# The seventh tile's logits and routing, moved from two to six steps into the eighth tile's matmuls

## Chip, cores and metric

The kernel runs on one core of a Trainium2 chip. The metric is the device time of one execution in microseconds (us).

## The reference, cut to what matters

Three stages follow each other: attention over two sequences of 576 tokens, a dense MLP with a cosine gate, and a second MLP in which every token goes to one of eight experts. The change lies where the second matmul of the dense MLP meets the routing of the second MLP.

```python
h = x @ w_in                      # 1152 x 512 by 512 x 2048
g = h * np.cos(h)
x = g @ w_out                     # 1152 x 2048 by 2048 x 512
logits = x @ w_gate               # 1152 x 8
expert_idx = np.argmax(logits, axis=1)
...
if counts[e] < capacity:
    disp[e, counts[e]] = x[i]     # token i takes the next place of its expert
...
h = np.maximum(np.einsum('ecd,edf->ecf', disp, w1), 0.0)
y = np.einsum('ecf,efd->ecd', h, w2)
out[i] = gate_w[i] * y[expert_idx[i], pos[i]]
```

## The kernel before, in words

The 1152 tokens are nine tiles of 128, counted here as first to ninth; the code counts them T = 0 to 8. `l2_wide` does the matmuls of `g @ w_out` for the first five tiles together. `l2r` does the other four one after the other and lays the routing of all nine tiles in between. A tile has 48 matmuls (L867, three for each of 16 blocks), which `l2r` takes in eight steps of six. After them `l2_end` empties the bank: ACT writes the row (L858) and, for the eighth and ninth tile, also a 32-bit copy `xq` (L856); DVE writes the row's low half (L859).

Routing a tile has two parts.

- `route_a` turns the tile. For the first seven tiles SP issues a transposing DMA, `xr` from `row` (L895). For the eighth and ninth (T >= NDT, NDT = 7), TensorE transposes `xq` (L900) and ACT copies the result (L902).
- `route_b` forms the logits on TensorE (L917 with `xr`, L914 with `xq`); DVE finds the largest (L927, L929, L930) and the one-hot row `roh` (L931); TensorE sums the places (L934 to L936); ACT forms the probability (L928, L937); DVE finds the row number `rsli` (L938 to L942), the weight (L943 to L945) and the new counts `cnt` (L946); POOL scatters the row to the table `disp` in device memory with an indirect DMA (L947).

In `l2r` a tile's `route_b` comes at the first step that lies at least `RD` = 2 steps behind its `route_a`. The seventh tile's `route_a` stands at step 16 (of 0 to 31), which is the first step of the eighth tile. Before the eighth tile's `route_b` stands `hook`: it copies the counts (L1310), and SP fetches the first 144 rows of two experts back from `disp`, turned (`eX`, L1013), with their weights and token numbers (`eM`, L1020). These fetches wait until the seventh tile's scatter has landed. After the eighth tile's `route_b`, `partial` picks the next expert (L1166 to L1175), and SP loads its number into a register (L1170).

Experts are worked in slots. The weights of a slot are eight chunks of 512 KB, fetched on SP's queue into the staging buffers `ws` (L969 for w1, L973 for w2), and each is split by ACT (L658) and then by DVE (L659) into two halves. There are three staging buffers here, so that a chunk is fetched when the chunk three places before it has been split. The chunks of the second slot are called 1 to 8 below, those of the third slot 9 to 16. Behind chunk 8 SP's queue holds the fetches of `hook`, then the register load L1170, then chunk 9.

Behind the ninth tile's matmuls TensorE starts on the two experts' first 144 rows: 12 matmuls a block (L1044), eight blocks for the first expert, then four for the second, then the first expert's second layer (L1066, four blocks of 24). A block takes the next of six PSUM banks (tags s, pt and mm, two of each); ACT (L1046) and DVE (L1047) empty it. In between lie the ninth tile's routing and `counts` (L1181 to L1206), which needs the ninth tile's `cnt`. Then comes a branch by size, and the rest of the experts.

The Python text gives the order in which work is issued. The framework's scheduler then sets the row of instructions on each engine by its own estimate of times, and every engine works its row in that order.

Of the kernel before, what the change touches and what calls it, by code (L numbers as in the profile page):

```python
# [51 lines left out]
MR = 8  # L52
RP = 2
RD = 2
RF = 2
W2P = 24
CYCLE = (
# [13 lines left out]
NDT = 7  # L71
# [6 lines left out]
def kernel(ctx, tc, q, k, v, s, w_in, w_out, wg, w1, w2, out, cap, wide):  # L78
# [802 lines left out]
    def l2(tiles):  # L881
        for T in tiles:
            xp = bank(L2T) if T == tiles[0] else bank("mm")
            for f in range(KF):
                l2_mm(xp, T, f)
                if f % 2 == 1:
                    if f == KF - 1:
                        l2_end(T, xp)
                    yield

    def route_a(T):
        r, xf = rows[T]
        if T < NDT:
            xr = work.tile([128, 2 * KD, 128], F16, tag="xr", name="xr", bufs=2)
            nc.sync.dma_start_transpose(out=xr, in_=r[:, 0:DM].bitcast(F16))  # L895
            rows[T] = (r, xr)
        else:
            tp = bank("pt")
            for kk in range(KD):
                nc.tensor.transpose(tp[:, kk * 128:(kk + 1) * 128], xf[:, kk * 128:(kk + 1) * 128], idf)  # L900
            xt = xq[:, DM:2 * DM].rearrange("p (k t) -> p k t", k=KD)
            nc.scalar.copy(xt.rearrange("p k t -> p (k t)"), tp)  # L902
            rows[T] = (r, xt)
# [103 lines left out]
    def e_rows(e, ns, rows_):  # L1007
        i = eb["n"]
        eb["n"] += 1
        n16 = -(-ns // 16) * 16  # L1010
        xo = i % XR * 2 * KD * 224 if ns <= 224 else i % 2 * 2 * KD * n16
        X = eb["X"][:, xo:xo + 2 * KD * n16].rearrange("p (k n) -> p k n", k=2 * KD)
        nc.sync.dma_start_transpose(out=X, in_=rows_[0:n16, 0:DM].bitcast(F16))  # L1013
        ex_[e] = (X, i)
# [8 lines left out]
    def at(src, off, ns):  # L1023
        n16 = -(-ns // 16) * 16
        return disp[bass.ds(src * NS if off is None else off, n16), :]
# [63 lines left out]
    def run(*gens):  # L1089
        live = [[g, n, 0.0] for g, n in gens]  # L1090
        while live:
            live.sort(key=lambda z: z[2])
            z = live[0]
            try:
                next(z[0])
                z[2] += 1.0 / z[1]
            except StopIteration:
                live.remove(z)

    def take(gen, n):  # L1100
        for _ in range(n):
            next(gen, None)
            yield

    def seq(*gens):
        for g in gens:
            yield from g

    def l2r(tiles, hook):
        gen = l2(tiles)  # L1110
        pend = list(range(tiles[0]))
        mid = []
        step = 0

        def finish():
            R_ = mid.pop(0)[0]
            if R_ == HTILE:
                hook()
            route_b(R_)
            if R_ in (PTILE, HTILE):  # L1120
                partial()

        for T in tiles:
            for j in range(KF // 2):
                next(gen)
                if mid and step - mid[0][1] >= RD:
                    finish()
                if pend and step % RP == 0:
                    mid.append((pend[0], step))
                    route_a(pend.pop(0))  # L1130
                step += 1
                yield
            pend.append(T)
        for T in pend:
            while mid and len(mid) >= 1:
                finish()
            mid.append((T, step))
            route_a(T)
        yield
        finish()  # L1140
        yield
# [15 lines left out]
    def partial():  # L1157
        V = nc.vector
        pp = bank("sm", 2)
        nc.tensor.matmul(pp[:, 0:E], lhsT=onesm, rhs=cnt[:, 0, :], start=True, stop=True)  # L1160
        ky = work.tile([1, E], F32, tag="ky", name="ky", bufs=1)
        so = work.tile([1, E], F32, tag="so", name="so", bufs=1)
        si = work.tile([1, 1], I32, name="psi", bufs=2)
        pick, keys = P["pick"], P["keys"]
        i = len(P["o"])
        V.scalar_tensor_tensor(ky, pp[0:1, 0:E], float(E), keys, ALU.mult, ALU.add)  # L1166
        V.max(so, ky)
        V.tensor_copy(si, so[:, 0:1])
        V.tensor_scalar(si, si, E - 1, E - 1, ALU.bitwise_and, ALU.bitwise_xor)
        P["o"].append(nc.values_load(si, engines=SP, min_val=0, max_val=E - 1))  # L1170
        if i < NH:
            V.tensor_copy(P["row"][:, i:i + 1], si)
            V.tensor_scalar(P["row"][:, i:i + 1], P["row"][:, i:i + 1], float(NS), None, ALU.mult)
        V.tensor_scalar(pick[:, i, :], ky, so[:, 0:1], None, ALU.is_equal)
        V.scalar_tensor_tensor(keys, pick[:, i, :], -1e9, keys, ALU.mult, ALU.add)  # L1175
# [121 lines left out]
    with ExitStack():  # L1297
        if True:
# [10 lines left out]
            def hook():  # L1309
                nc.vector.tensor_copy(cnt0, cnt[:, 0, :])  # L1310
                for h in range(NH):
                    e_rows(h, HEAD, at(P["o"][h], None, HEAD))
                    e_meta(h, HEAD, at(P["o"][h], None, HEAD))

            def ahead(steps):
# [6 lines left out]
                while k < 2 * items:  # L1322
                    next(pre)
                    k += 1

            tail = l2r(range(WN, NTILE), hook)
            lead = (NTILE - WN) * KF // 2 + 1
            run((take(tail, lead), lead), (ahead(lead), lead))
            ws[0:0] = [xa.tile([128, 1024], F32, name=f"ws{3 + i}") for i in range(NST)]
            phase, phase1 = (expert(h, HEAD, "out0", ex_.pop(h)) for h in range(NH))  # L1330
            for _ in range(RF):
                next(phase)
# [5 lines left out]
            for h in range(NH):  # L1338
                n = max(p[h] for p in PROFILES)
                e_rows(h, n, at(P["o"][h], first[h], n))  # L1340
            run((seq(take(phase, KE - RF), take(phase1, LA), phase, phase1), 2 * (KE + KD)), (take(pre, items), W3P))
            level = nc.values_load(regs[0], min_val=0, max_val=len(LIMITS))
# [42 lines left out]
```

## Time and profile before

| | us |
|---|---|
| median of three runs | 432.86 |
| lowest and highest of them | 428.65, 433.86 |
| the profiled execution | 430.29 |
| its span in the trace | 428.2 |
| PE busy | 395.1 (92%) |
| DVE busy | 311.8 (73%) |
| ACT busy | 274.8 (64%) |
| POOL busy | 149.2 (35%) |

The profiled execution's time is its span and 2.1 us that lie around it. PE is TensorE's matmuls, DVE the vector engine, ACT the scalar engine, POOL GpSimd, SP the engine whose queue issues the DMAs. The shares are means over a program whose stages have different limits; the stage of the change lies between 264 and 325 us of the span.

### The profile page before, as it was taken

The page shows a single profiled execution, that of the slowest core. Times are in us where ns is not written, and L with a number is a line of the kernel's source. Part 1 is how long each engine was busy: PE and PEld are TensorE (multiplying, and loading weights), DVE is VectorE, ACT ScalarE, POOL GpSimd, SP SyncE. Part 2 cuts the span into 40 slices and gives each one's busy share as a digit, 9 for nine tenths or more (in the row PEclk, how much of TensorE's full clock was granted, in tenths as well). Part 3 has the DMA queues.
Part 4 walks back from the last instruction along what each step waited for, and adds up shares of the span by engine and source line. Part 5 has one row for each costly group of instructions (what it writes and reads, how often), then busy time and mean ns, then how long its engine had stood idle before and what let it go on. Part 6 is the DMA issues. An engine that isn't in the chain of part 4 may idle for free.

```text
span 428.2 us, 10640 instructions
## 1 busy us (share of the span) xinstructions
PE 395.1 (92%) x3928; PEld 281.6 (66%) x3928; DVE 311.8 (73%) x768; ACT 274.8 (64%) x630; POOL 149.2 (35%) x261
## 2 busy tenths in 40 slices
PE   2799999999999999999999999797998999999783
PEld 2588888886666666654444454354997999987552
DVE  7769999749999599989885664672842477877670
ACT  6679989986878677775234532533734477777560
POOL 7668887563554445455000032010011011122100
PEclk9989999999999999999999999899999999999998
DMA  7979795203369932323667456947759298998851
GB/s 166 210 173 190 165 203 151 72 2 100 98 188 328 369 124 92 88 70 98 183 204 230 116 128 206 280 110 222 252 148 216 61 314 264 308 330 265 264 209 30
DMA packets 90003, 77.38 MB, mean 181 GB/s; under 512 B 62768, under 2 KB 70960, under 8 KB 89942
## 3 DMA queue, kind: packets, MB, share of 16 engines
q1 hardware_dynamic: 86934, 71.62, 59.5%
q0 software_dynamic: 1952, 4.73, 3.2%
q8 instruction: 33, 0.54, 0.5%
q10 hardware_dynamic: 1056, 0.26, 0.3%
q14 instruction: 28, 0.23, 0.2%
HBM read 57.66 MB, written 12.28 MB: 163 GB/s over the span
## 4 chain that ended last, share of the span: by engine, by line
PE 32%; DMA 9%; DVE 7%; issue 5%; ACT 4%; SPq 2%; POOL 1%; POOLq 0%; ACTq 0%; DVEq 0%
DMA ws<-in_moe_w_dram 8%; PE ps_mm L867 7%; PE ps_sm L867 5%; PE ps_pt L1044 3%; PE ps_s L1066 3%; PE ps_mm L1044 2%; PE ps_s L867 2%; PE ps_pt L867 2%; PE ps_s L1044 2%; PE ps_pt L1066 2%; PE ps_mm L1066 2%; DVE gall L659 1%; ACT gall L658 1%; DVE y L818 1%; SPq L1013 1%
## 5 line engine op out<-in xcount | busy, mean ns | idle before, releaser
L812 PEld LDWEIGHTS <-win 128*128 128x128 f16 x576 | 56.3, 98 | 37.0
L867 PEld LDWEIGHTS <-gall 128*128 128x128 f16 x432 | 41.3, 98 | 49.3 <-issue 2.5
L867 PE MATMUL ps_mm<-wout,gall 128*128 128x512 f16 x240 | 57.9, 387 | 0.3 <-DVE n__2954 L826 0.3
L659 DVE SCALAR_TENSOR_TENSOR gall<-ws,gall 128x1024 f16<-128x1024 f32 x32 | 38.8, 1221 | 23.2 <-ACT gall L658 22.1
L1053 POOL DMA_INDIRECT out_dram<-gall,eM x15 | 18.8, 1252 | 98.4 <-ACT gall L1052 77.4
L658 ACT ACTIVATE gall<-ws 128x1024 f16<-128x1024 f32 x32 | 33.7, 1056 | 26.8 <-DMA ws<-in_moe_w_dram 26.8
L658 ACT ACTIVATE wout<-ws 128x512 f16<-128x512 f32 (+1 forms) x32 | 27.3, 860 | 23.7 <-DVE ws L681 18.5
L241 ACT ACTIVATE z<-z,st 128x256 f32<-128x256 f32 (+4 forms) x72 | 41.9, 586 | 0.7 <-DVE st L241 0.7
L947 POOL DMA_INDIRECT disp<-row,rsli x9 | 9.2, 1017 | 94.0 <-ACT rm L928 48.5
L241 DVE CUSTOM_DVE_ANT_0 z<-ps_s,zm 128x512 f32<-128x512 f32 (+3 forms) x72 | 34.5, 511 | 10.0 <-PE ps_s L244 8.8
L659 DVE SCALAR_TENSOR_TENSOR wout<-ws,wout 128x512 f16<-128x512 f32 (+1 forms) x32 | 30.4, 955 | 8.2 <-ACT wout L658 8.0
L812 PE MATMUL ps_s<-xT,win 128*128 128x384 f16 x192 | 34.2, 326 | 0.0
L812 PE MATMUL ps_pt<-xT,win 128*128 128x384 f16 x192 | 33.8, 326 | 0.0
L812 PE MATMUL ps_mm<-xT,win 128*128 128x384 f16 x192 | 33.8, 326 | 0.0
L247 PE MATMUL ps_pt<-idf,z 128*128 128x128 f32 x192 | 30.2, 282 | 1.3 <-DVE p L241 1.3
L1044 PEld LDWEIGHTS <-gall 128*128 128x128 f16 x480 | 27.0, 97 | 3.7 <-issue 1.9
L825 ACT ACTIVATE y<-y,quarter 128x384 f32<-128x384 f32 x48 | 29.2, 609 | 0.1
L241 ACT COPY p<-ps_pt 128x512 f32<-128x512 f32 (+2 forms) x48 | 25.2, 525 | 5.9 <-PE ps_pt L247 5.5
L659 DVE SCALAR_TENSOR_TENSOR win<-ws,win 128x1024 f16<-128x1024 f32 x16 | 19.4, 1225 | 11.7 <-ACT win L658 11.7
L247 PEld LDWEIGHTS ps_pt<-idf,z 128*128 128x128 f32 x192 | 23.1, 144 | 6.3 <-issue 1.5
L244 PE MATMUL ps_s<-kT,qT 128*128 128x384 f16 (+7 forms) x128 | 23.9, 307 | 1.1 <-DMA kT<-bt 0.6
L658 ACT ACTIVATE win<-ws 128x1024 f16<-128x1024 f32 x16 | 16.8, 1055 | 10.9 <-DMA ws<-in_moe_w_dram 10.9
(495 smaller groups left out, 891.9 us busy)
## 6 DMA issues: line engine op xcount, KB each, us to landing
ws<-in_moe_w_dram SPq DMA_DIRECT2D x64, 512.0 KB
ws<-in_moe_w_in_dram SPq DMA_DIRECT2D x16, 512.0 KB
ws<-in_moe_w_out_dram SPq DMA_DIRECT2D x16, 512.0 KB
disp<-zc SPq DMA_DIRECT2D x18, 257.0 KB
out_dram<-zc SPq DMA_DIRECT2D x9, 256.0 KB
qf<-in_q_dram SPq DMA_DIRECT2D x16, 128.0 KB
vf<-in_v_dram SPq DMA_DIRECT2D x16, 128.0 KB
kf<-in_k_dram SPq DMA_DIRECT2D x14, 128.0 KB
```

The lines of the kernel that those rows point to most:

```text
L241: return pin(f(*a, **kw))
L244: return pin(nc.tensor.matmul(out_, **kw))
L247: return pin(nc.tensor.transpose(out_, in_, id_))
L658: nc.scalar.activation(hi, src, AF.Copy, scale=sc)
L659: (eng or nc.vector).scalar_tensor_tensor(lo, src, sc, hi, ALU.mult, ALU.subtract)
L812: nc.tensor.matmul(hp[:, 0:CH], lhsT=win[a][:, kk, fs], rhs=xT[:, x_, kk, xs], start=(n == 0), stop=(n == 3 * KD - 1))
L825: nc.scalar.activation(y, y, AF.Sin, scale=TWO_PI, bias=quarter)
L867: gate["pe"] = nc.tensor.matmul(xp, lhsT=G[c][:, a, f, ts], rhs=wout[w_][:, f, :], start=(f == 0 and n == 0), stop=(f == KF - 1 and n == 2))
L947: sc = nc.gpsimd.indirect_dma_start(out=disp, out_offset=bass.IndirectOffsetOnAxis(ap=sli.bitcast(U32), axis=0), in_=r, in_offset=None, bo ...
L1044: gate["pe"] = nc.tensor.matmul(hp[:, 0:ns], lhsT=a1[:, kk, a, fs], rhs=X[:, x_ * KD + kk, 0:ns], start=(n == 0), stop=(n == 3 * KD - 1))
L1053: sc = nc.gpsimd.indirect_dma_start(out=out, out_offset=bass.IndirectOffsetOnAxis(ap=M[:, b, 1:2].bitcast(U32), axis=0), in_=y, in_offset= ...
L1066: nc.tensor.matmul(yp[:, 0:ns], lhsT=a2[:, f, w_, d * 128:(d + 1) * 128], rhs=Hh[:, a, f, :], start=(n == 0), stop=(n == 3 * KE - 1))
```

## The change

For the seventh tile alone (T = NDT - 1), `route_b` comes six steps behind `route_a` and not two, so at step 22 in place of step 18. Nothing is added or left out.

```diff
 RD = 2
+RL = 6
 RF = 2
...
                 next(gen)
-                if mid and step - mid[0][1] >= RD:
+                if mid and step - mid[0][1] >= (RL if mid[0][0] == NDT - 1 else RD):
                     finish()
```

The new line shifts the numbers behind it by one, so that L659 before is L660 after. On TensorE's row the seventh tile's twelve logit matmuls stand behind 24 matmuls counted from the place where the row of before has its L934, and not behind 7. The scheduler then orders DVE, ACT and POOL anew between this place and the branch; SP's row stays as it was, instruction for instruction.

DVE, the seventh tile's routing from the one-hot row on. Before:

```order
L931 TENSOR_SCALAR roh<-rw,rm 128x8
L946 TENSOR_TENSOR cnt<-cnt,roh 128x8
L1310 COPY cnt_84<-cnt 128x8
L938 TENSOR_SCALAR rt_3894<-ps_sm 128x8
L659 SCALAR_TENSOR_TENSOR gall<-ws_92,gall 128x2x512
L939 TENSOR_TENSOR rt_3894<-rt_3894,ps_sm 128x8
L943 TENSOR_SCALAR rm<-rm 128x1
L940 TENSOR_TENSOR rt_3894<-rt_3894,roh 128x8
L944 RECIPROCAL rm<-rm 128x1
L942 TENSOR_REDUCE rsli<-rt_3894 128x1
L659 SCALAR_TENSOR_TENSOR gall<-ws_90,gall 128x2x512
L945 TENSOR_SCALAR row<-rm 128x1
```

And in the changed kernel:

```order
L660 SCALAR_TENSOR_TENSOR gall<-ws_91,gall 128x2x512
L932 TENSOR_SCALAR roh<-rw,rm 128x8
L944 TENSOR_SCALAR rm<-rm 128x1
L860 SCALAR_TENSOR_TENSOR row<-ps_mm,row 128x512
L939 TENSOR_SCALAR rt_3918<-ps_sm 128x8
L945 RECIPROCAL rm<-rm 128x1
L947 TENSOR_TENSOR cnt<-cnt,roh 128x8
L940 TENSOR_TENSOR rt_3918<-rt_3918,ps_sm 128x8
L946 TENSOR_SCALAR row<-rm 128x1
L660 SCALAR_TENSOR_TENSOR gall<-ws_92,gall 128x2x512
L941 TENSOR_TENSOR rt_3918<-rt_3918,roh 128x8
L943 TENSOR_REDUCE rsli<-rt_3918 128x1
```

Before, the splits in this piece are those of chunks 5 (ws_92) and 6 (ws_90), and 7 and 8 come behind it. Now the split of chunk 7 (ws_91) stands ahead of the one-hot row, and the split of chunk 8 (the second ws_92) ahead of the last two steps to the row number `rsli`, without which POOL can't scatter.

ACT, from the last tile's 32-bit copy `xq` on. Before:

```order
L658 ACTIVATE gall<-ws_90 128x1024
L856 ACTIVATE xq<-ps_mm 128x512
L858 ACTIVATE row<-ps_mm 128x512
L658 ACTIVATE gall<-ws_91 128x1024
L902 COPY xq<-ps_pt 128x512
L658 ACTIVATE gall<-ws_92 128x1024
L1046 ACTIVATE eH<-ps_s 128x144
```

And in the changed kernel:

```order
L857 ACTIVATE xq<-ps_mm 128x512
L859 ACTIVATE row<-ps_mm 128x512
L903 COPY xq<-ps_pt 128x512
L1047 ACTIVATE eH<-ps_s 128x144
L659 ACTIVATE gall<-ws_90 128x1024
L1047 ACTIVATE eH<-ps_pt 128x144
```

The splits of chunks 9 to 11 (ws_90, ws_91, ws_92 here) stood ahead of the ninth tile's three evacuations and the first expert block's; now these four come first.

DVE, around the release of the first experts' banks. Before:

```order
L659 SCALAR_TENSOR_TENSOR gall<-ws_92,gall 128x1024
L1047 SCALAR_TENSOR_TENSOR eH<-ps_s,eH 128x144
L1047 SCALAR_TENSOR_TENSOR eH<-ps_pt,eH 128x144
L930 TENSOR_REDUCE rm<-rw 128x1
L943 TENSOR_SCALAR rm<-rm 128x1
L1047 SCALAR_TENSOR_TENSOR eH<-ps_mm,eH 128x144
L931 TENSOR_SCALAR roh<-rw,rm 128x8
L659 SCALAR_TENSOR_TENSOR gall<-ws_90,gall 128x1024
```

And in the changed kernel:

```order
L660 SCALAR_TENSOR_TENSOR gall<-ws_92,gall 128x1024
L943 TENSOR_REDUCE rsli<-rt_4130 128x1
L946 TENSOR_SCALAR row<-rm 128x1
L1191 MAX so<-ky 1x8
L1195 TENSOR_TENSOR pr<-ps_sm,pick 1x8
L1192 CAST si<-so 1x8
L1195 TENSOR_TENSOR pr<-ps_sm,pick 1x8
L1193 TENSOR_SCALAR si<-si 1x8
L1197 TENSOR_TENSOR pr<-ps_sm,pick 1x8 x3
L1198 COPY ky<-so 1x5
L1048 SCALAR_TENSOR_TENSOR eH<-ps_mm,eH 128x144
L660 SCALAR_TENSOR_TENSOR gall<-ws_90,gall 128x1024
```

Both pieces go from the split of chunk 11 to that of chunk 12. Before, three expert blocks are emptied in between and the ninth tile's counts come later; now the counts' arithmetic stands there, and only the third block (bank mm) is emptied. Elsewhere on this row the ninth tile's `cnt` now stands behind the split of chunk 9, and the second expert's first four blocks behind those of chunks 13 to 16; before, two of the four came ahead of chunk 13.

## Rows read from the trace of the kernel before

**Rows 1.** Stretches: us, then PE, PEld, DVE, ACT, POOL busy, clock, DMA share, GB/s.

```profile
271.50:274.10 2.60, 0.01 (x1) 0.00 (x0) 0.60 (x1) 1.03 (x1) 0.00 (x0) 1.00 1.08 306
274.50:277.50 3.00, 3.00 (x12) 1.08 (x9) 1.90 (x7) 1.99 (x5) 0.00 (x0) 0.50 0.95 266
...
293.70:296.70 3.00, 0.05 (x2) 0.02 (x1) 0.52 (x1) 1.61 (x3) 0.00 (x0) 1.00 0.93 329
296.70:306.80 10.10, 10.09 (x149) 9.80 (x150) 9.39 (x45) 6.89 (x17) 0.97 (x1) 1.00 0.88 280
340.70:410.00 69.30, 62.90 (x855) 56.36 (x851) 49.60 (x73) 49.88 (x91) 12.09 (x8) 1.00 0.88 288
```

**Rows 2.** Timeline of PE: start, us, instruction, count, [idle before <- releaser].

```profile
263.10 6.85 PE L867 MATMUL ps_mm<-wout,gall 128*128 128x512 f16 x31
269.79 0.17 PE L934 MATMUL ps_sm<-ebrow,onesm 128*128 128x16 f16 x1
...
274.13 0.46 PE L917 MATMUL ps_s<-wgs,xr 128*128 128x8 f16 x12 [2.62 <-ACT gall L658]
274.45 3.77 PE L867 MATMUL ps_mm<-wout,gall 128*128 128x512 f16 x9
278.05 0.17 PE L936 MATMUL ps_sm<-roh,tri 128*128 128x16 f16 x1
...
282.83 2.75 PE L867 MATMUL ps_mm<-wout,gall 128*128 128x512 f16 x12
...
292.82 0.91 PE L1044 MATMUL ps_s<-eX,win 128*128 128x144 f16 x12
296.68 0.65 PE L900 MATMUL ps_pt<-idf,xq 128*128 128x128 f32 x4 [2.95 <-ACT xq L856]
...
306.06 0.91 PE L1044 MATMUL ps_mm<-eX,gall 128*128 128x144 f16 x12
306.81 1.66 PE L1066 MATMUL ps_s<-eH,win 128*128 128x144 f16 x24
```

**Rows 3.** The chain that ended last, 281 to 297 us: start, us, what.

```profile
281.12 0.16 DVE row L945
...
282.08 3.22 DMA disp<-row,rsli
...
285.38 2.24 SPq L1013
...
291.45 3.62 DMA ws<-in_moe_w_dram
...
296.05 0.59 ACT xq L856
```

**Rows 4.** Timeline of ACT, same columns as rows 2.

```profile
275.70 1.06 ACT L658 ACTIVATE gall<-ws 128x1024 f16<-128x1024 f32 x1
...
279.06 1.06 ACT L658 ACTIVATE gall<-ws 128x1024 f16<-128x1024 f32 x1 [0.98 <-DMA ws<-in_moe_w_dram]
...
283.33 1.06 ACT L658 ACTIVATE gall<-ws 128x1024 f16<-128x1024 f32 x1 [0.94 <-DMA ws<-in_moe_w_dram]
...
299.13 1.06 ACT L658 ACTIVATE gall<-ws 128x1024 f16<-128x1024 f32 x1 [0.59 <-DMA ws<-in_moe_w_dram]
```

**Rows 5.** Timeline of DVE, same columns.

```profile
274.15 1.23 DVE L659 SCALAR_TENSOR_TENSOR gall<-ws,gall 128x1024 f16<-128x1024 f32 x1 [2.06 <-ACT gall L658]
...
278.37 1.22 DVE L659 SCALAR_TENSOR_TENSOR gall<-ws,gall 128x1024 f16<-128x1024 f32 x1
...
304.15 0.16 DVE L942 TENSOR_REDUCE rsli<-rt 128x1 int32<-128x8 f32 x1
...
304.97 0.29 DVE L1047 SCALAR_TENSOR_TENSOR eH<-ps_pt,eH 128x144 f16<-128x144 f32 x1
...
309.08 4.61 DVE L659 SCALAR_TENSOR_TENSOR gall<-ws,gall 128x1024 f16<-128x1024 f32 x4
```

**Rows 6.** SP's own waits, 324 to 341 us: us in total, times, longest.

```profile
SPq L1013 <- PE ps_pt L1044: 7.5, 2, 4.9
```

## The prediction

> **What bounds the kernel now.** I read the busy table by stretch first, then PE's timeline, then the chain that ended last, then ACT and DVE in the same stretch. The reader is to see two pauses of PE. From 271.5 to 274.1 it does nothing [rows 1]: it stands before the seventh tile's logits, which wait for the transposing DMA of `xr`; they start at 274.13 after 2.62 us [rows 2]. Behind this pause the granted clock is 0.50 from 274.5 to 277.5 [rows 1], and nine matmuls take from 274.45 to 278.05, 3.60 us [rows 2]. The second pause, 2.95 us before 296.68, ends with ACT's `xq` L856 [rows 2]; after it the clock stays at 1.00 [rows 1].
>
> The chain says why the second one is there [rows 3]. DVE finishes the seventh tile's row at 281.28, POOL's scatter starts at 282.08 and lands 3.22 us on, SP's fetch of `eX` starts at 285.38 and, behind it on the queue, that of chunk 9 at 291.45; chunk 9 is there at about 295.1, and ACT, which has its split ahead of the ninth tile's `xq`, only then comes to the `xq` at 296.05. So what binds here is a line of waits through DVE, POOL and SP's queue, and the seventh tile's scatter is its head. From 296.7 to 306.8 PE is busy 10.09 of 10.10 us [rows 1].
>
> **What the change takes away.** 31 matmuls start within 263.10 to 269.79 [rows 2], 0.216 us each. The logits now stand 24 matmuls behind 269.79: 269.79 + 24 x 0.216 = 274.97. SP's row is unchanged, so `xr` still lands at about 274.13, 0.84 us earlier. The first pause (2.62 us) goes, and with it the nine slow matmuls' excess, 3.60 - 9 x 0.216 = 1.66 us. On ACT the ninth tile's evacuations now come ahead of chunk 9, so the second pause (2.95 us) goes too. Sum: 7.2 us of PE time. It counts only where nothing else is late.
>
> **What is late next: the scatter.** Each engine works its row in order, so I follow DVE's new row. Chunk 7 may be fetched when chunk 4 is split; that split starts at 274.15 and stays, so ACT still starts on chunk 7 at 279.06 [rows 4, 5], and DVE splits it from 280.15 to 281.38 (1.06 and 1.23 us). Now the one-hot row stands behind this split: 281.5. The eighth tile's `xq`, also behind chunk 7 on ACT, starts at 280.0. PE has done the six matmuls of the ninth tile that stand ahead of the transposes by 277.9, waits for `xq` until 280.65, and again for the one-hot row until 281.6, because L936 now stands among the transposes. So PE comes back to the ninth tile at 281.95, not 282.83 [rows 2]: of the 4.3 us that the first pause and its slow matmuls gave, 0.9 are left.
>
> DVE goes on: the eighth tile's row half (0.69 us), five small steps to 282.6, then the split of chunk 8. Its fetch follows the split of chunk 5, which DVE started at 278.37 [rows 5], behind a step that waited for PE. Nothing of the routing stands ahead of it now, and ACT began on chunk 5 at 275.70 or earlier [rows 4], so DVE starts between 275.4 and 276.8; I take 276.3. Before, 283.33 - 279.59 = 3.74 us lay between that split's end and ACT on chunk 8 [rows 4, 5]. So chunk 8 lands at about 281.3, ACT has it by 282.4, DVE splits it from 282.6 to 283.85, and the row number is ready at 284.15 (284.6 with the later chunk 5). POOL's scatter follows a finished row by 0.80 us (281.28 to 282.08) [rows 3]: 284.95, which is 2.9 us later than 282.08. Bounds: 0.8 us later at least, since the logits start 0.84 us later; 4 at most, if chunk 8 lands as late as before, 283.33.
>
> SP's queue behind it moves as a whole: the fetches of `eX`, the register load and chunk 9 come 2.9 us later, chunk 9 at 298.0. Queued behind that are chunks 10 to 16, and for each of them ACT, DVE and all that stands behind the split on DVE.
>
> **What PE then waits for.** The ninth tile ends at about 291.9. When `eX` lands no row shows; it is between its issue at 285.38 [rows 3] and the first use at 292.82 [rows 2], so now between 288.3 and 295.7; I take 292.8, by the 4.5 us that `xr` took. Five expert blocks, the transposes and the ninth logits (some 5 us of PE) bring it to 298, or 300.9 at the latest. There stands the sum over the counts (L1181), which needs the ninth tile's `cnt`, behind the split of chunk 9 on DVE: 298.0 + 1.06 + 1.23 + four small steps = 300.85. PE waits 2 to 3 us, which also covers a late `eX` and a slow clock in the ninth tile.
>
> Then three blocks at 0.75 us (306.06 to 306.81) [rows 2] to 303.1. The second expert's first block needs the bank mm of the third block, which DVE now empties behind chunks 10 and 11 and the counts' arithmetic. Chunk 11 came 299.13 - 295.09 = 4.0 us behind chunk 9 on ACT [rows 3, 4]: 302.0, split on DVE by 304.35. The arithmetic takes 304.97 - 304.15 = 0.82 us [rows 5], the emptying 0.25. PE waits from 303.1 to 305.45. The next block waits for chunk 12's split (to 306.6) until 307.0; the four are done at 309.25. Before, they were done at 306.81 [rows 2].
>
> The second layer's first two blocks take 1.5 us each, and nine matmuls of the fourth are drawn ahead (0.56): 312.8. The third needs the bank of the second expert's first block, now emptied behind chunks 13 to 16, whose four splits take 4.61 us [rows 5]; they start at about 308.8, so the bank is free at 313.7. PE waits 0.9 us, then 24 + 15 matmuls (2.4 us): 316.1. Before, the layer started at 306.81 and took four times 1.5 us, to 312.8. **The difference at this place is +3.3 us.**
>
> **What becomes of it.** From there the rows of both kernels are the same. From 324 to 341 SP's next fetches wait for PE's blocks (7.5 us in two waits for the tag pt) [rows 6], so the weights' stream comes later with PE; from 340.7 to 410 the DMA engines are 0.88 busy [rows 1], and I see no slack that gives 3 us back. The end comes 3.3 us later: 430.29 + 3.3 = 433.6 against the profiled execution. That execution is 2.6 us below the median of 432.86; from the median it would be 436.2. I take the middle, 435.0.
>
> **The clock.** Of two pauses of similar length one was followed by the half clock and one was not [rows 1]. The forecast has new pauses of some 3, 2.4 and 0.9 us behind 297; each may cost another 1.66 us, or nothing. The Trainium skill ("TensorE: Matmul & The Clock Gate", Part 1: The HAM clock gate) says that how many matmuls run slowly differs from run to run of one kernel; this trace, with its two pauses, agrees. By that rule the end lies 3.3 to 8.3 us later, and the forecast takes the lower end as the row of the longer pause shows it.
>
> **Rivals.**
>
> - The scatter is hardly later (0 to 0.8 us). For it: chunk 8 may land earlier than I think, and DVE may then be through in time. Against it: chunk 7's split alone holds the one-hot row until 281.5. All later waits hang on chunk 9, so the difference shrinks to 3.3 - 2.9 = 0.4 up to 1.2 us: 431 to 434, no change.
> - Most of the 7.2 us is kept, because the banks come free sooner than the row of DVE suggests. For it: PE has no other work in the way. Against it: three waits that all need a weight chunk. With the first pause's 4.3 us kept: 427 to 428; with all of it 423 to 425.
> - Slower by more than I say: the half clock follows the waits at L1181, at the bank mm and at the bank of the second layer. It decides from the second such pause on: 3.3 + 2 x 1.66 = 6.6, with three 8.3 us, so 437 to 441; with a scatter 4 us late 9.4, over 2%.
> - The change doesn't do what it says: `xr` lands behind 274.97 and PE still waits there. The first pause's rest would be short (the margin is 0.84 us), and the line through the scatter only grows by it: the forecast's time.
>
> **How the numbers follow.** Forecast (1.2 to 6 us later, with the last rival in it) 0.58; hardly later scatter 0.18; gain kept 0.10; slower clock 0.14. Two per cent, 8.6 us, is about what a measurement of this kernel can tell from no change. Faster by that needs all 7.2 us and more: 0.03. Slower by that needs the top of the third rival: 0.08. Within: 0.89. The range goes from 428.0, which leaves out most of the kept gain, to 441.0, the third rival with three slow stretches and the forecast's base.
>
> **What would show each step.** Right: no wait before the seventh tile's logits (start near 275); the scatter of its rows near 285; SP's `eX` near 288; chunk 9 on ACT near 298 with the ninth tile's `xq` ahead of it; a wait of PE at L1182 (L1181 before) that DVE's `cnt` ends, and one at the second expert's first block that DVE's emptying of a bank ends. Wrong: a scatter at 283 or earlier, or PE without waits from 293 to 309; then the gain is kept and the kernel is faster. A granted clock of 0.50 in several stretches behind 298 would be the slower rival.

## The result, and the profile after

| | before | after |
|---|---|---|
| median (20 runs each), us | 431.0 | 435.29 |
| lowest and highest, us | 428.04, 434.26 | 430.87, 439.78 |
| the profiled execution, us | 430.29 | 436.88 |

The ratio is 1.0091, with a 95% interval of 1.0064 to 1.0119. It leaves disturbed runs out, so it is not quite the quotient of the medians. The change costs some 3.9 us (0.91% of 431.0).

The profiled execution of after is later than that of before already ahead of the change: the sixth tile's logits, the last ones that stand at the same place in both, start at 261.64 before and at 263.85 after. So 2.21 us are taken off the times of after wherever they are compared with the prediction; the frames show them as they are. TensorE's timeline, first that one row of before, then after:

```profile
261.64 0.45 PE L917 MATMUL ps_s<-wgs,xr 128*128 128x8 f16 x12
```

```profile
263.85 0.45 PE L918 MATMUL ps_s<-wgs,xr 128*128 128x8 f16 x12
...
265.62 12.03 PE L868 MATMUL ps_mm<-wout,gall 128*128 128x512 f16 x55
277.49 0.45 PE L918 MATMUL ps_s<-wgs,xr 128*128 128x8 f16 x12
...
282.55 0.55 PE L901 MATMUL ps_pt<-idf,xq 128*128 128x128 f32 x3 [1.96 <-ACT xq L857]
283.47 0.17 PE L937 MATMUL ps_sm<-roh,tri 128*128 128x16 f16 x1 [0.36 <-DVE rm L944]
...
295.32 0.79 PE L1045 MATMUL ps_s<-eX,win 128*128 128x144 f16 x10
...
301.46 0.17 PE L1182 MATMUL ps_sm<-cnt,onesm 128*128 128x8 f16 x1 [0.30 <-DVE cnt L947]
...
307.38 0.95 PE L1045 MATMUL ps_mm<-eX,gall 128*128 128x144 f16 x12 [3.52 <-DVE eH L1048]
308.83 1.60 PE L1045 MATMUL ps_s<-eX,gall 128*128 128x144 f16 x12 [0.50 <-DVE eH L1048]
310.22 1.55 PE L1045 MATMUL ps_pt<-eX,gall 128*128 128x144 f16 x12
...
312.36 1.66 PE L1067 MATMUL ps_s<-eH,win 128*128 128x144 f16 x24
...
316.50 1.66 PE L1067 MATMUL ps_mm<-eH,win 128*128 128x144 f16 x24 [0.42 <-DVE eH L1048]
```

The reader is to see that both pauses of [rows 2] are gone, 2.62 us before the seventh tile's logits and 2.95 us before the ninth tile's transposes, and that others have come behind them. The longest, 3.52 us, stands before the second expert's first block. The busy table of after says what the clock did (columns as in [rows 1]):

```profile
268.00:277.50 9.50, 9.50 (x46) 4.31 (x45) 5.41 (x5) 4.60 (x5) 0.67 (x3) 1.00 0.95 299
...
284.00:288.00 4.00, 4.00 (x14) 1.59 (x11) 1.90 (x10) 0.97 (x2) 0.98 (x1) 0.57 0.01 4
...
303.86:307.38 3.52, 0.00 (x0) 0.00 (x0) 2.36 (x14) 2.65 (x5) 0.00 (x0) 1.00 0.77 203
308.80:311.60 2.80, 2.77 (x24) 2.77 (x24) 2.80 (x16) 1.23 (x3) 0.51 (x1) 0.51 1.05 401
...
342.90:412.20 69.30, 63.84 (x918) 58.40 (x915) 48.92 (x74) 49.48 (x95) 12.27 (x9) 1.00 0.86 265
```

Two pauses are followed by the half clock, the lower of TensorE's two levels (1.2 and not 2.4 GHz): the one at 280.6 (0.57 from 284 to 288) and the one at 303.86 (0.51 from 308.8 to 311.6). The line through the scatter, on DVE, POOL, SP's queue and ACT:

```profile
282.05 1.22 DVE L660 SCALAR_TENSOR_TENSOR gall<-ws,gall 128x1024 f16<-128x1024 f32 x1 [0.54 <-ACT gall L659]
283.19 0.22 DVE L932 TENSOR_SCALAR roh<-rw,rm 128x8 f16<-128x8 f32 x1
...
284.53 1.22 DVE L660 SCALAR_TENSOR_TENSOR gall<-ws,gall 128x1024 f16<-128x1024 f32 x1
...
285.86 0.16 DVE L943 TENSOR_REDUCE rsli<-rt 128x1 int32<-128x8 f32 x1
...
305.02 1.23 DVE L660 SCALAR_TENSOR_TENSOR gall<-ws,gall 128x1024 f16<-128x1024 f32 x1 [2.00 <-ACT gall L659]
...
307.04 0.29 DVE L1048 SCALAR_TENSOR_TENSOR eH<-ps_mm,eH 128x144 f16<-128x144 f32 x1
```

```profile
286.84 0.98 POOL L948 DMA_INDIRECT disp<-row,rsli  x1 [18.17 <-DVE rsli L943]
```

```profile
290.01 1.30 SPq L1014 DMA_TRANSPOSE eX<-disp  x1
...
295.11 6.24 SPq L970 DMA_DIRECT2D ws<-in_moe_w_dram  x4
```

```profile
295.52 0.60 ACT L857 ACTIVATE xq<-ps_mm 128x512 f32<-128x512 f32 x1 [5.73 <-PE ps_mm L868]
...
298.68 1.06 ACT L659 ACTIVATE gall<-ws 128x1024 f16<-128x1024 f32 x1 [1.03 <-DMA ws<-in_moe_w_dram]
...
303.93 1.06 ACT L659 ACTIVATE gall<-ws 128x1024 f16<-128x1024 f32 x1 [2.08 <-DMA ws<-in_moe_w_dram]
```

Chunk 7's split ends and the one-hot row follows; chunk 8's split ends and the row number follows. The scatter is 2.55 us later than in [rows 3] (284.63 against 282.08), `eX` 2.42, chunk 9 on ACT 1.38 (296.47, against 295.09 in this row of ACT's timeline of before). Behind the split of chunk 11 (303.93 on ACT, 305.02 on DVE) and the counts' arithmetic DVE comes at 307.04 to the bank that TensorE waits for. The row of ACT of before:

```profile
295.09 1.06 ACT L658 ACTIVATE gall<-ws 128x1024 f16<-128x1024 f32 x1 [7.80 <-DMA ws<-in_moe_w_dram]
```

### The profile page after: what moved, and what is told of

The parts are those of the page before. It is cut to its first block, busy times and chain, and to the rows that moved or that the text cites. A ratio compares the mean times of both kernels' runs of the same rounds, so it can differ in the third digit from the quotient of the medians.

```text
span 434.9 us, 10643 instructions
## 1 busy us (share of the span) xinstructions
PE 397.3 (91%) x3928; PEld 282.2 (65%) x3928; DVE 312.0 (72%) x768; ACT 275.5 (63%) x630; POOL 149.7 (34%) x261
## 5 line engine op out<-in xcount | busy, mean ns | idle before, releaser
L868 PEld LDWEIGHTS <-gall 128*128 128x128 f16 x432 | 41.6, 99 | 50.0 <-issue 3.2
L660 DVE SCALAR_TENSOR_TENSOR gall<-ws,gall 128x1024 f16<-128x1024 f32 x32 | 39.1, 1222 | 19.7 <-ACT gall L659 19.1
L659 ACT ACTIVATE gall<-ws 128x1024 f16<-128x1024 f32 x32 | 33.8, 1056 | 23.5 <-DMA ws<-in_moe_w_dram 22.4
L659 ACT ACTIVATE wout<-ws 128x512 f16<-128x512 f32 (+1 forms) x32 | 27.3, 861 | 23.3 <-DVE ws L682 18.6
L660 DVE SCALAR_TENSOR_TENSOR wout<-ws,wout 128x512 f16<-128x512 f32 (+1 forms) x32 | 30.5, 955 | 7.9 <-ACT wout L659 7.7
L1045 PEld LDWEIGHTS <-gall 128*128 128x128 f16 x480 | 28.4, 100 | 8.1 <-issue 6.3
L248 PE MATMUL ps_pt<-idf,z 128*128 128x128 f32 x192 | 29.3, 276 | 1.3 <-DVE p L242 1.3
L660 DVE SCALAR_TENSOR_TENSOR win<-ws,win 128x1024 f16<-128x1024 f32 x16 | 19.5, 1224 | 11.7 <-ACT win L659 10.8
L659 ACT ACTIVATE win<-ws 128x1024 f16<-128x1024 f32 x16 | 16.8, 1054 | 10.8 <-DMA ws<-in_moe_w_dram 10.8
```

The source lines that it names most:

```text
L248: return pin(nc.tensor.transpose(out_, in_, id_))
L659: nc.scalar.activation(hi, src, AF.Copy, scale=sc)
L660: (eng or nc.vector).scalar_tensor_tensor(lo, src, sc, hi, ALU.mult, ALU.subtract)
L868: gate["pe"] = nc.tensor.matmul(xp, lhsT=G[c][:, a, f, ts], rhs=wout[w_][:, f, :], start=(f == 0 and n == 0), stop=(f == KF - 1 and n == 2))
L1045: gate["pe"] = nc.tensor.matmul(hp[:, 0:ns], lhsT=a1[:, kk, a, fs], rhs=X[:, x_ * KD + kk, 0:ns], start=(n == 0), stop=(n == 3 * KD - 1))
```

## The experiments

Four theories were tried. A: the line from the row number over the scatter and SP's queue to chunk 9 sets the end, and the change loses because two splits now stand in it. A2: part of the loss comes from banks that DVE empties behind later splits. B: a late place of the logits costs by itself. C: the half clock after new pauses is the loss. All kernels stand against the kernel before, which ran beside them; each ratio of e1 to e12 comes from 12 runs. The edits are shown against the changed kernel, cut with `...`.

The table gives, from one profiled execution each, how much later (us) than before four places are: the scatter (before 282.08), the first `eX` fetch (285.38), chunk 9 on ACT (295.09) and the first expert's second layer (306.81). As for after, the lateness of the sixth tile's logits has been taken off.

| kernel | scatter | `eX` | chunk 9 | layer | ratio, 95% |
|---|---|---|---|---|---|
| the change | +2.55 | +2.42 | +1.38 | +3.34 | 1.0091 (1.0064 to 1.0119) |
| e1 late row number | +3.27 | +3.58 | +2.80 | +2.82 | 1.0074 (1.0037 to 1.0111) |
| e2 hold 7, 8 | +0.10 | +0.14 | -0.98 | +1.84 | 0.9988 (0.9948 to 1.0028) |
| e3 blocks first | +3.02 | +2.76 | +2.52 | +1.91 | 1.0040 (1.0002 to 1.0079) |
| e4 three steps | -0.08 | +0.04 | -0.41 | +0.54 | 0.9976 (0.9940 to 1.0012) |
| e5 hold 5 to 8, six steps | -1.48 | +0.91 | +0.06 | +0.62 | 1.0045 (1.0009 to 1.0081) |
| e6 the same, two steps | -1.07 | -0.41 | -1.36 | -0.70 | 0.9922 (0.9894 to 0.9951) |
| e7 e5 and blocks | -1.51 | +0.93 | +0.39 | +1.31 | 1.0004 (0.9964 to 1.0044) |
| e8 hold 8 | +1.33 | +1.54 | +0.65 | +1.38 | 1.0026 (0.9989 to 1.0063) |
| e9 hold 5 to 8, four steps | -2.34 | -1.43 | -2.23 | -1.72 | 0.9970 (0.9932 to 1.0007) |
| e10 e6 with filled pause | -1.75 | +0.94 | +6.21 | +6.16 | 1.0062 (1.0013 to 1.0110) |
| e11 turned by TensorE | -5.22 | -2.08 | -2.66 | -2.71 | 0.9945 (0.9908 to 0.9981) |
| e12 hold 5 to 8, three steps | -2.31 | -1.53 | -2.60 | -2.19 | 0.9977 (0.9943 to 1.0011) |

**e1: the row number late.** The logits stay two steps behind; one DVE step is queued behind a later split.

```diff
-RL = 6
+RL = 2
-        with nc.allow_low_precision(...):
+        with nc.allow_low_precision(...), (tc.issue_after(gate["c"].ins) if T == NDT - 1 else ExitStack()):
             V.tensor_reduce(sli, t1, AX.X, ALU.add)
```

Here `gate["c"]` is the last split issued on DVE, that of chunk 8.

> The logits stay where they were before (two steps behind); only the step that finishes the seventh tile's row number stands behind the split of chunk 8 on DVE. Theory A (the line row number, scatter, SP's queue, chunk 9, DVE sets the end): the scatter starts 4 to 4.5 us later than before, the kernel is 3 to 5 us slower than before (ratio 1.007 to 1.012), although PE's place of the logits is untouched. Theory B (the place of the logits among the matmuls sets it): ratio 0.998 to 1.002. Theory C (half clock after the new pauses of the change): ratio near 1.000 unless new half-clock stretches show.

The scatter came 3.27 us later (4 to 4.5 expected) and the ratio is 1.0074, in A's range. Up to the experts' blocks nothing was moved on TensorE, so the loss needs no late logits (B). It isn't the late row number alone, however: from there on the scheduler gave TensorE, DVE and ACT another order than before. TensorE now waits for a step of the ninth tile that DVE has behind the split of chunk 9, and for a bank that DVE empties behind that of chunk 12:

```profile
304.05 0.17 PE L937 MATMUL ps_sm<-roh,tri 128*128 128x16 f16 x1 [3.22 <-DVE rm L944]
...
310.82 0.91 PE L1045 MATMUL ps_s<-eX,gall 128*128 128x144 f16 x12 [1.76 <-DVE eH L1048]
```

**e2 and e8: the change with splits held back.** A split is issued on DVE only behind the seventh tile's row number. In e2 this holds chunks 7 and 8, in e8 (with `items + 7`) chunk 8 alone.

```diff
-            V.tensor_reduce(sli, t1, AX.X, ALU.add)
+            i_ = V.tensor_reduce(sli, t1, AX.X, ALU.add)
+        if T == NDT - 1:
+            gate["r6"] = i_
...
-                after("ev cnt", split, ...)
+                after("r6 ev cnt", split, ...)
...
-                    if i > KF // 2 + 1 and k < min(...):
+                    if i > KF // 2 + 1 and k < min(...) and (k < items + 6 or "r6" in gate):
```

> The logits stand six steps behind as in the change, but the splits of chunks 7 and 8 are held behind the seventh tile's row number on DVE. Theory A: the first pause of PE is gone, the scatter starts about 1.4 us earlier than before (near 280.7 on the clock of the trace of before), and the kernel is 1 to 2 us faster than before (ratio 0.995 to 0.998), some 5 us faster than the changed kernel. Theory B: like the changed kernel, ratio 1.007 to 1.012. Theory C: like the changed kernel if half-clock stretches stay behind 284 and 308, otherwise 1.4 us better than it (1.005).

> The change as it is, with one split alone moved: that of chunk 8 stands behind the seventh tile's row number. Chunk 7's still stands ahead of the one-hot row. Theory A: the scatter starts 0.5 to 1.2 us later than before (2.5 in the change), and most of the loss is gone: ratio 0.999 to 1.004. Theory B: 1.007 to 1.012 as in the change.

With the logits still six steps behind, holding one split takes the ratio from 1.0091 to 1.0026, holding two to 0.9988. Where the two splits stand that the prediction named decides the loss, and B in its full size is refuted: six steps without the loss. Holding the splits also changed the order of the experts' blocks (see below), so the path of the loss is not shown by this alone. A was too hopeful on e2: the scatter came at +0.10, not 1.4 us early, because DVE had the one-hot row behind chunk 6, and TensorE waited for it (e2's timeline), and a later pause was followed by the half clock (e2's busy table):

```profile
283.26 0.17 PE L937 MATMUL ps_sm<-roh,tri 128*128 128x16 f16 x1 [2.42 <-DVE roh L932]
```

```profile
299.20:307.80 8.60, 8.60 (x77) 8.52 (x78) 6.13 (x13) 5.47 (x14) 0.00 (x0) 0.60 0.77 244
```

8.60 us at 0.60 are some 3.4 us more than at 1.00 (8.60 x 0.40, an estimate). That is enough to put this execution, one of the longest of e2's twelve (435.58 us, median 433.97), at +1.84 in the layer although chunk 9 came 0.98 us early.

**e3: more blocks ahead of the ninth tile's routing.** `RF` is the count of the first expert's blocks that are issued there.

```diff
-RF = 2
+RF = 4
```

> The change as it is, but two more steps of the first expert's blocks are issued ahead of the ninth tile's routing, so that DVE empties the banks ahead of the splits of chunks 10 to 12. The scatter is as late as in the change. Theory A in its narrow form (all is lost at chunk 9's arrival): ratio 1.007 to 1.012 as in the change. Theory A2 (the loss is the emptying of the banks behind the splits: PE's 3.5 us wait at the second expert's first block): that wait falls under 1 us and the ratio is 0.999 to 1.006. Theory B: as in the change.

The 3.52 us wait went, and waits of 0.59, 1.16 and 0.17 us at other blocks and one of 1.98 us at the counts came, all ended by DVE; their sum, 3.90 us, is no smaller. Then the half clock followed: the layer's first block took 3.03 us, not 1.66.

```profile
302.10 0.72 PE L1045 MATMUL ps_pt<-eX,win 128*128 128x144 f16 x9 [0.59 <-DVE eH L1048]
303.98 0.91 PE L1045 MATMUL ps_s<-eX,win 128*128 128x144 f16 x12 [1.16 <-DVE eH L1048]
306.00 0.41 PE L1045 MATMUL ps_pt<-eX,gall 128*128 128x144 f16 x4 [0.17 <-DVE eH L1048]
310.09 0.17 PE L1182 MATMUL ps_sm<-cnt,onesm 128*128 128x8 f16 x1 [1.98 <-DVE cnt L947]
310.63 3.03 PE L1067 MATMUL ps_s<-eH,win 128*128 128x144 f16 x24
```

The ratio, 1.0040, lies in A2's range, but its interval overlaps that of the change. By the two ratios the order in which the banks are emptied would hold some half of the loss; that is not settled.

**e4: three steps.** `RL = 3`.

> The logits stand three steps behind and not two; DVE's row is that of before. Theory A: the scatter starts 0 to 0.3 us later than before, PE's pause before the logits is 1.3 us and not 2.6, and nothing is gained or lost behind it: ratio 0.998 to 1.002. Theory B (a later place is worse in proportion): a quarter of the change's loss, 1.002 to 1.003. If PE's pause itself counted: 1.3 us and part of its slow matmuls gained, 0.995 to 0.997.

The expected 1.3 us pause didn't come; TensorE paused 2.52 us. The row of instructions says why: three steps put the logits where two did, 38 wide matmuls behind the tile before, and only two small matmuls (L935, L936) stand elsewhere. On the other engines no instruction has moved. So e4 is in effect the kernel before once more, and its 0.9976 shows how far a ratio of 12 runs strays. It tells nothing of A or B.

**e5, e6, e9, e12: the whole routing ahead of chunks 5 to 8.** The edit of e2 with `items + 4`, and `RL` = 6, 2, 4 and 3. The rows of DVE are the same in the last three.

> Six steps as in the change, but the whole routing of the seventh tile stands on DVE ahead of the splits of chunks 5 to 8. Theory A (the line row number, scatter, SP's queue, chunk 9 sets the end): the scatter starts 3 to 4 us earlier than before, neither pause of PE (2.6 and 2.95 us) is left, the kernel is 2.5 to 5 us faster than before (ratio 0.988 to 0.994). Theory B (the late place of the logits costs by itself): 1.007 to 1.012 as in the change. A third way, the weights' stream already full from 300 us on: 0.995 to 1.000 in spite of an earlier scatter.

> The logits two steps behind, as before, with the same hold of chunks 5 to 8 behind the row number. The scatter is as early as in the kernel with six steps or up to 0.8 us earlier, but PE keeps its 2.6 us pause before the logits and the slow matmuls behind it. Theory A in its pure form (the line alone counts, the pause is hidden): within 1 us of the kernel with six steps and the same hold. If PE's pause counts once the line is short: 2 to 4 us slower than that kernel, ratio 0.995 to 1.000.

> The hold of chunks 5 to 8 behind the row number, with the logits four steps behind and not two or six. DVE's row is that of the kernel with two steps and the same hold; on TensorE 12 matmuls more stand ahead of the logits' tail and the sum over the one-hot row stands 5 matmuls behind the logits, not 9. Theory A: the pause before the logits is 1 to 1.8 us and not 2.65, the scatter as early as with two steps or up to 1 us earlier, chunk 9 on ACT 1 to 2 us earlier than before; ratio 0.988 to 0.994. Theory B (each step of lateness costs, 1.2% over four steps): 0.996 to 1.000, halfway between two and six steps.

> The same hold of chunks 5 to 8 and the same rows of DVE as with two and with four steps, the logits three steps behind. Theory A: the scatter 1 to 2.3 us and chunk 9 on ACT 1.3 to 2.3 us earlier than before, between the kernels with two and with four steps, ratio 0.991 to 0.997. Theory B (lateness of the logits costs by itself, some 0.25% a step): between 0.992 and 0.997 too, but above two steps and below four by the time alone, with no order in the trace that explains it. A ratio at or under that of two steps speaks against B; one at or over that of four steps (0.997) leaves it open.

e5 is a miss: the scatter came 1.48 us early, `eX` still 0.91 us late, and the kernel is slower (1.0045, the interval wholly over 1). DVE had the one-hot row at 276.66, then stood for ACT's `rex`, which ACT had behind chunk 6; chunk 5's split stands behind that, so chunk 8 was fetched late, and the scatter took 5.6 us to land beside it. Chunk 9 itself is on time (+0.06), so the line up to chunk 9 doesn't make this loss. First DVE of e5, then the rows of DMA issues from 278 to 290 us of e5, e6 and after (count, then us from issue to landing):

```profile
276.66 0.23 DVE L932 TENSOR_SCALAR roh<-rw,rm 128x8 f16<-128x8 f32 x1
279.24 0.15 DVE L946 TENSOR_SCALAR rm<-rm 128x1 f32<-128x1 f32 x1 [2.34 <-ACT rex L938]
```

```profile
disp<-row,rsli POOLq DMA_INDIRECT x1, 5.6
```

```profile
disp<-row,rsli POOLq DMA_INDIRECT x1, 3.9
```

```profile
disp<-row,rsli POOLq DMA_INDIRECT x1, 3.1
```

e6 has the routing nearly as early, `eX` and chunk 9 early too, and TensorE keeps its pause there (2.65 us). It was expected within 1 us of e5 or slower, and is 1.2% faster: a second miss. e12 is the same program as e6 but for the place of the two small matmuls, as e4 is to before. So 0.9922 and 0.9977 are two measurements of one order of work, in the mean 0.995: some 0.5% faster than before, twice what e4 strays, and 1.4% faster than the change. The pause that the change removes is not what a faster kernel has to lose. The mean granted clock of the 12 runs, 0.9907 in e6 and 0.9883 in e12, goes the same way as the two ratios.

e9 is the only one of the three whose logits really come later (five wide matmuls). Its scatter and chunk 9 are as early as e12's, its ratio (0.9970) lies between those of the other two: no cost of lateness by itself (B) shows here. A small one is not excluded: by the ranges set beforehand e9 lies in B's (0.996 to 1.000) and not in A's (0.988 to 0.994), and e12's value leaves B open. At six steps (e5) `eX` is late again, by ACT's `rex` and by chunk 8, and the experts' blocks have another order, so e5 doesn't tell B from A.

**e7: e5 with one more step of blocks** (`RF = 3`).

> The hold of chunks 5 to 8 behind the row number with six steps, and one more step of the first expert's blocks ahead of the ninth tile's routing. If the emptying of the banks behind the weight splits (A2) still costs something with an early scatter: 0.5 to 2 us faster than without the extra step. If chunk 9 comes early enough: the same within 0.5 us. If the later counts cost more: 0.5 to 1.5 us slower.

1.0004 against e5's 1.0045; the intervals overlap, so this tells nothing for or against A2.

**e10: the pause filled.** e6 with idle matmuls ahead of the seventh tile's logits, in the same bank (`lb_`).

```diff
+            if T == NDT - 1:
+                c, j = divmod(T + 1, TPC)
+                for _ in range(20):
+                    nc.tensor.matmul(lb_, lhsT=G[c][:, 0, KF - 1, j * 128:(j + 1) * 128], rhs=wout[0][:, KF - 1, :], start=True, stop=True)
```

> Two steps and the hold of chunks 5 to 8, and 20 idle matmuls of 128 x 512 (their result is overwritten) issued on TensorE ahead of the seventh tile's logits, where it paused 2.65 us. Theory C (the half clock after the pause costs time on the line, because the sum over the one-hot row stands behind the slow matmuls): the granted clock stays at 1.00 in the 4 us behind the logits (0.57 without the filling), the row number comes 1 to 1.7 us earlier, and the kernel is 0 to 2 us faster than without the filling: ratio 0.987 to 0.993. If the pause has nothing to do with the clock: still 0.5 to 0.6 there, ratio 0.992 to 0.997, since the filling adds 1.7 us to PE.

The busy tables of e6 (with the pause) and of e10 behind the logits:

```profile
276.00:279.50 3.50, 3.50 (x12) 1.30 (x10) 1.86 (x7) 2.42 (x5) 0.00 (x0) 0.53 0.84 307
```

```profile
276.70:281.00 4.30, 3.76 (x30) 1.85 (x31) 2.32 (x8) 2.32 (x5) 0.00 (x0) 1.00 0.99 336
```

The clock stayed at 1.00, as C said; but e12 kept 1.00 behind an unfilled pause of 2.88 us (last section), so this doesn't show that the filling did it. And the kernel is slower: in the new order ACT has chunk 8 ahead of the eighth tile's `xq`, waits 5.14 us for it, and TensorE 3.56 us for the `xq`. This is the second pause of [rows 2] one tile earlier. The profiled execution took 440.19 us, where the median of the twelve is 436.81, so its +6.16 is above the usual loss.

```profile
287.68 1.06 ACT L659 ACTIVATE gall<-ws 128x1024 f16<-128x1024 f32 x1 [5.14 <-DMA ws<-in_moe_w_dram]
288.64 0.58 ACT L857 ACTIVATE xq<-ps_mm 128x512 f32<-128x512 f32 x1
```

**e11: the seventh tile turned by TensorE.** `RL = 2`, `NDT = 6`: the seventh tile gets the 32-bit copy and TensorE's transposes, as the eighth and ninth do.

> Two steps, and the seventh tile turned by TensorE from a 32-bit copy, as the eighth and ninth are, not by the transposing DMA: the logits wait for no DMA. The row number stands on DVE behind chunk 4's split and ahead of chunk 5's. Theory A: the scatter starts 1 to 3 us earlier than before, chunk 9 on ACT 0.5 to 2.5 us earlier, ratio 0.988 to 0.996. If the copies that this adds on ACT (1.2 us) hold the splits of chunks 3 to 5 instead: 0.998 to 1.004.

The scatter came 5.22 us early, but `eX` only 2.08: the scatter took 6.4 us to land, with DMA engines 0.72 busy in that time. It is faster (0.9945, the interval wholly under 1), as much as e6 and e12 in the mean.

```profile
disp<-row,rsli POOLq DMA_INDIRECT x1, 6.4
```

```profile
278.53:284.97 6.44, 6.21 (x31) 2.94 (x30) 4.00 (x5) 4.14 (x6) 2.24 (x2) 1.00 0.72 204
```

**A rival that no run settles: the order of the experts' blocks.** Behind the moved steps the scheduler set not only DVE, ACT and POOL anew but also TensorE's row in the experts' blocks. The rows of the traces fall into two kinds. In e2, e4, e6, e9, e10, e11 and e12 DVE's row from the eighth tile's routing on is that of before, and but for e2 so is TensorE's from the first expert block on; their ratios are 0.9922 to 0.9988, e10 apart. In the change, e1, e3, e5, e7 and e8 both rows are others; their ratios are 1.0004 to 1.0091. So the order may cost by itself: every edit that kept the change's late row number had another order too. For the line speak e6 and e11, with the order of before, chunk 9 early and the interval wholly under 1; e1, whose layer is as late as its chunk 9 (2.82 and 2.80); and e10, with the order of before, a late chunk 9 and a loss, though TensorE is late there already ahead of it. For the order speaks e5, slower with chunk 9 on time. In the change the layer is 1.96 us later than chunk 9, of which two blocks at half clock are 1.28. How the 3.9 us divide stays open.

**How much the clock costs.** The runs are listed with their mean granted clock. Over the 20 runs of after it is 0.9847, over the four sets of before that stand beside the experiments 0.9858 to 0.9870. Within these five sets a run at 0.01 less takes 1.8 to 3.5 us longer (a straight line through the runs, r -0.44 to -0.72). So C accounts for 0.2 to 0.8 us of the change's 3.9, an estimate: by it the clock is a part of the loss and not the greater one.

## Why the prediction was right, point by point

- **The first pause goes.** Right: no wait before the logits, start 275.28 (forecast 274.97). The nine slow matmuls went with it.
- **New waits at `xq` and the one-hot row.** Right: until 280.34 and 281.26 (280.65 and 281.6).
- **Coming back.** The forecast had the ninth tile end at 291.9; the first expert's first block starts at 293.11, against 292.82 in [rows 2]. The half clock followed the pause (0.57), where the kernel before had 1.00 from 282 to 288, so all of the 4.3 us were lost here, not 3.4.
- **The scatter.** Right: one-hot row 281.2 (281.5), row number 283.8 (284.15), scatter 2.55 us late (2.9). That the late row number is the cause was argued in the prediction; e2 and e8 show that the loss goes with the two splits, all of it and most of it. That it goes by way of the scatter, and not of the order behind it, is not shown.
- **SP's queue moves as a whole.** The step that failed in size. `eX` came 2.42 us late, chunk 9 only 1.38 (forecast 2.9): the first `eX` issue held SP's queue 1.30 us, not 2.24 as in [rows 3].
- **The wait at the counts (L1182), 2 to 3 us.** It was 0.30: chunk 9 came sooner and TensorE later than forecast.
- **The wait at the second expert's first block, 2.4 us until 305.45.** Right in place and end (305.17), the end by luck: chunk 9 came on ACT 1.5 us sooner than forecast, but chunk 11 5.25 us behind it (303.93 - 298.68) and not 4.0. The wait was 3.52 us long, because TensorE had not waited at the counts.
- **The first layer's end.** 309.25 forecast, 310.15 measured (+3.34 against [rows 2]): the two blocks at half clock took 1.39 us apiece, not 0.75, so 1.28 us more. This is the third rival, once.
- **The second layer.** Bank free at 314.29 (313.7), wait 0.42 us (0.9); the layer ends at 316.73 (318.00 + 15 x 0.0625 - 2.21), 3.9 us late against a forecast of 3.3.
- **What becomes of it.** Right: the DMA engines are 0.86 busy from 342.9 to 412.2, and nothing is given back. The span ends 434.9 - 2.21 - 428.2 = 4.5 us later in this execution, 3.9 us by the ratio.
- **The time.** The median is 435.29; 435.0 was forecast. That it is so near is luck: the base in the forecast, 431.7 (435.0 - 3.3), is 0.7 us over the 431.0 of 20 runs, and the step of 3.3 us is 0.6 under the 3.9 by the ratio. Smaller differences than the two per cent of the prediction can also be told: the interval keeps 0.9% clear of no change.

The rivals: the scatter was not early; the 7.2 us were not kept; `xr` landed in time. The slower clock came in part, as above. The prediction reads a spread from run to run off two pauses of a single run; what bears it out is e6 and e12, one order of work with 0.53 and 1.00 behind like pauses (last section).

## What to carry to other kernels

Moving a step later to hide its wait also moves everything that hangs on its result; follow the longest line behind it first (here a row number, a scatter, a queue, a weight chunk). Where every engine works its row in order, look at which long steps the scheduler puts ahead of the short steps of that line: two splits of 1.22 us there, with the order of work that came with them, cost more than the pause of 2.62 us that was removed. Holding the splits of chunks 5 to 8 behind the short steps, with the logits left where they were, came out faster than both kernels (0.9922 and 0.9977 in two measurements, the second within its interval of no change); filling the pause without looking at ACT's row was a loss. And an edit that moves one step lets the scheduler order others anew, so compare the rows of all engines before a difference is put down to that step.

## What was not expected of the hardware

- The scatter of one tile landed 3.1 us after its issue where the DMA engines were 0.22 busy (after) and 5.6 and 6.4 us where it ran beside a weight chunk and they were 0.54 and 0.72 busy (e5, e11). So an earlier scatter gains less than it is early. The Trainium skill ("DMA: Bandwidth & Descriptors", Queues, rings and completion order) says that a DMA engine takes turns between the queues that have work for it; these three numbers agree with that, and no run here shows the turns themselves.
- Pauses of the same length are not followed by the same clock. With the same order of work e6 paused 2.65 us and then had 0.53 (1.2 GHz nearly throughout); e12 paused 2.88 us and kept 1.00 (timeline of e6, then timeline and busy table of e12):

```profile
275.55 0.46 PE L918 MATMUL ps_s<-wgs,xr 128*128 128x8 f16 x12 [2.65 <-DMA xr<-row]
```

```profile
276.49 0.46 PE L918 MATMUL ps_s<-wgs,xr 128*128 128x8 f16 x12 [2.88 <-DMA xr<-row]
```

```profile
276.00:280.00 4.00, 3.51 (x28) 1.80 (x29) 3.13 (x14) 2.60 (x6) 0.00 (x0) 1.00 0.75 277
```

One profiled execution therefore shows differences that another of the same work doesn't have: the scatter is at -1.07 in e6 and at -2.31 in e12, the layer at -0.70 and -2.19.
